# First operands loaded from one array in the order of use, on one queue, in smaller pieces; warming matmuls on a program constant

## The chip, the cores and the metric

The kernel runs on one core of one Trainium2 chip. The metric is the device time of one execution in microseconds (us), lower is better. It was run three times before the change: 705.35, 705.52 and 707.34 us, median 705.52.

## What is computed

`x` has 2048 rows (the sequence) and 512 columns. Two branches of `x` are mixed by a gate per row:

```python
g = sigmoid((x * gate_w).sum(-1, keepdims=True))
# branch A: the real part of a DFT over columns and then over rows, as matrix products
a = einsum("bsd,ed->bse", x, dft_hid_re);  b = einsum("bsd,ed->bse", x, dft_hid_im)
A = einsum("ts,bse->bte", dft_seq_re, a) - einsum("ts,bse->bte", dft_seq_im, b)
# branch B: a gated MLP of width 1376
B = einsum("bsf,fd->bsd", silu(x @ w1) * (x @ w3), w2)
out = g * A + (1 - g) * B
```

All inputs and the output are float32.

## The kernel before

Every product of matrices is made as three matmuls of 128x128 by 128x512: each operand is split into a high part (rounded to the matmul's format, names ending in `h`) and a low part (what is left, names ending in `l`), and high times high, high times low and low times high are added up in PSUM. ScalarE (ACT in the profile) makes the high part by a copy (L63), VectorE (DVE) the low part by a subtraction (L64). Matrices are cut into 2x2 blocks `B11` to `B22`, and seven products of sums of blocks, `P1` to `P7`, take the place of eight. The program has three large stages. First the DFT over the columns (PSUM tiles `dP`): `DSEQ` lists its 14 products, seven for each half `g` of the sequence, and begins with `P2` of half 0 and `P2` of half 1. Both need only the block `B21` of `x` (tiles `xB21_0` and `xB21_1`) and the block `B21` of the DFT matrix (`dB21`). Then comes the MLP (`X`, `Y`, `Z`), and last the DFT over the rows (`P`), whose end writes `out`.

A block is a tile of 128 partitions by 1024 numbers: two halves of 512, `q` = 0 and 1, which are the two steps of 128 of the contraction. `sums_of(s, (0,), True)` multiplies the first halves alone, before the second halves have arrived; with `first` set it runs all four matmuls of high by high, then the four of low by high, then the four of high by low, so that the low parts may come later (L186). Without it, each of the four row blocks takes its three matmuls in turn through `mm3` (L71). A matmul row in the profile reads "stationary names are the second, moving names the first": in `dP<-dB21h,x0B21h` four blocks of 128 columns of `x0B21h` are loaded in turn as weights, and 512 columns of `dB21h` are streamed through each.

The start of the program is what the change touches. `load_d("B21", ...)` loads `dB21` in two halves, the first on ACT's DMA queue, the second on SP's; `load_x(g, "B21", 2)` loads `xB21_0` and `xB21_1` in two halves each on SP's queue. On SP the order is: x0 first half, x1 first half, d second half, x0 second half, x1 second half, then the other blocks as whole tiles of 512 KB. The arrays lie in device memory as rows of 1024 numbers per partition, so a half is 128 pieces of 2 KB, 4 KB apart. While these loads run, TensorE has nothing of its own to do and multiplies a tile of zeros, `warm`, nine times (L793); VectorE fills that tile first (L790). Then the first half of `xB21_0` is split by VectorE alone (L114, L115), the others by ACT and VectorE in the order d, x1, d, x0, x1. Engines take their instructions in the order in which the program issues them; `keep_in_program_order` pins the order of the DMAs.

Of the kernel before, what the change touches and what calls it, by code (L numbers as in the profile page):

```python
# [16 lines left out]
G = 2  # L17
NC = (F + P - 1) // P
NP = (NC - 1) // 2
NQ = 4  # L20
WARM = 9


@with_exitstack
def fnet_swiglu_gate_kernel(
    ctx: ExitStack,
    tc: tile.TileContext,
    xt: bass.AP,
    cc: bass.AP,
    dd: bass.AP,  # L30
# [10 lines left out]
    nc = tc.nc  # L41
# [20 lines left out]
    def split(hi, lo, src):  # L62
        nc.scalar.activation(hi, src, AF.Copy)  # L63
        nc.vector.tensor_sub(lo, src, hi.bitcast(F32))  # L64

    def minus_sum(o, a, b):
        nc.vector.scalar_tensor_tensor(o, a, -1.0, b, op0=ALU.mult, op1=ALU.subtract)

    def mm3(ps, ah, al, bh, bl, first, last, chain=False):
        for n, (u, v) in enumerate(((ah, bh), (ah, bl), (al, bh))):  # L70
            nc.tensor.matmul(ps, u, v, start=first and n == 0, stop=last and n == 2,  # L71
                             skip_group_check=chain)
# [14 lines left out]
    act0 = const.tile([P, 24], F32, tag="act0", name="act0")  # L87
# [1 line left out]


    RX, RD, XF, WD = {}, {}, {}, {}
    XK = ("B11", "B21", "B12", "B22")

    def load_x(g, k, parts=1):
        RX[g, k] = raw(f"x{k}_{g}")
        for a in range(parts):
            n = slice(a * 1024 // parts, (a + 1) * 1024 // parts)
            yield tc.keep_in_program_order(nc.sync.dma_start(RX[g, k][:, n], xt[g, XK.index(k)][:, n]))

    def load_d(k, queues=(nc.sync,)):  # L100
        RD[k] = raw(f"d{k}")
        w = 1024 // len(queues)
        for a, queue in enumerate(queues):
            n = slice(a * w, (a + 1) * w)
            yield tc.keep_in_program_order(queue.dma_start(RD[k][:, n], dd[XK.index(k)][:, n]))

    def operand(src, name, parts=1, pool=op):
        tag = {op: "op", zo: "zo", f4: "f4"}[pool]
        h, l = (pool.tile([P, 1024], F32R, tag=tag, name=f"{name}{v}") for v in "hl")

        def piece(a, by_vector=False):
            n = slice(a * 1024 // parts, (a + 1) * 1024 // parts)
            if by_vector:
                nc.vector.tensor_copy(h[:, n], src[:, n])  # L114
# [4 lines left out]
        return (half(h), half(l)), [lambda a=a, **kw: piece(a, **kw) for a in range(parts)]  # L119

    def form_x(g, k, parts=1):
        r = {n: RX.get((g, n)) for n in ("B11", "B12", "B21", "B22", "F2", "F3")}
        if k == "F3":
            RX[g, k] = raw(f"xF3_{g}")
            nc.vector.tensor_add(RX[g, k], r["B12"], r["B22"])
# [9 lines left out]
        XF[g, k], pieces = operand(RX[g, k], f"x{g}{k}", parts)  # L135
        return pieces

    def form_d(k, parts=1):
        r = {n: RD.get(n) for n in ("B11", "B12", "B21", "B22", "v5", "v6")}
        if k == "v5":  # L140
            RD[k] = raw("dv5")
            nc.vector.tensor_sub(RD[k], r["B11"], r["B12"])
# [9 lines left out]
        WD[k], pieces = operand(RD[k], f"d{k}", parts, f4 if k in ("B22", "v4") else zo)  # L152
        return pieces

    PX = {"P2": ("B21", "B21"), "P1": ("B11", "B11"), "P5": ("F3", "v5"), "P6": ("F2", "v6"),
# [3 lines left out]
    def forms_of(s):  # L159

        if s < len(DSEQ):
            g, (xk, dk) = DSEQ[s][0], PX[DSEQ[s][1]]
            todo = form_x(g, xk) + (form_d(dk) if dk not in WD else [])
            for f in todo:
                f()

# [5 lines left out]
    def sums_of(s, qs=(0, 1), first=False):  # L172
        g, p = DSEQ[s]
        x, z = ((0, 1), (2, 3)) if g == 0 else ((2, 3), (0, 1))
        own = p in ("P1", "P2", "P5")
        if own and 0 in qs:
            ks = x if p == "P1" else z
            DP[g, p] = [pair(k, f"d{p}{g}{k}") for k in ks]
        ps = DP[g, {"P6": "P1", "P7": "P1", "P4": "P1", "P3": "P5"}.get(p, p)]
        xh, xl = XF[g, PX[p][0]]  # L180
        wh, wl = WD[PX[p][1]]
        if first:

            for n, (u, v) in enumerate(((xh, wh), (xl, wh), (xh, wl))):
                for i in range(4):
                    nc.tensor.matmul(ps[i // 2][:, i % 2], u[:, 0, i * P : (i + 1) * P], v[:, 0],  # L186
                                     start=n == 0, stop=False, skip_group_check=True)
# [38 lines left out]
    def load_w(c):  # L226
        WS[c] = raw(f"ws{c}")
        nc.sync.dma_start(WS[c], w13[c])

    def prep_wa(c):  # L230
        h, l = (zo.tile([P, 768], F32R, tag="zo", name=f"wa{c}{v}") for v in "hl")
        split(h, l, WS[c][:, :768])
        WA[c] = half(h, 3), half(l, 3)

    def sum_wb(c):
        w = half(WS[c], 4)
        u = raw(f"wu{c}")
# [222 lines left out]
    todo = list(INNER)  # L460
# [315 lines left out]

    def run(*gens):
        for gen in gens:  # L780
            for _ in gen:
                pass
# [7 lines left out]
    nc.vector.memset(warm, 0.0)  # L790
    wps = pair(0, "wps")
    for n in range(WARM):
        nc.tensor.matmul(wps[:, 0], warm[:, :P], warm, start=True, stop=True)  # L793
    nc.scalar.activation(act0[:, :1], warm[:, :1], AF.Silu)
    run(load_x(0, "B11"), load_d("B11"), load_x(0, "B12"), load_x(0, "B22"),
        load_d("B12"), load_d("B22"))
# [16 lines left out]
    def work(count):  # L813
        for _ in range(count):
            if later:
                later.pop(0)()

    tasks = {2: lambda: run(load_x(1, "B11")), 3: lambda: run(load_x(1, "B12")),
             5: lambda: run(load_x(1, "B22")), 6: lambda: run(load_x(1, "B21")),
             7: lambda: load_w(0), 9: lambda: sum_wb(0), 11: lambda: prep_wa(0),  # L820
             12: lambda: (prep_wb(0), load_w(1))}
# [65 lines left out]
    start = AT[2, "P1", 0]  # L887
# [73 lines left out]
```

## Time and profile before

| what | value |
|---|---|
| median of three runs | 705.52 us (705.35 to 707.34) |
| the profiled execution, its own time | 707.5 us |
| span of that execution, first to last instruction | 705.7 us |
| PE (matmuls) busy, share of the span | 699.7 us, 99% |
| VectorE busy | 565.1 us, 80% |
| ScalarE busy | 345.8 us, 49% |
| DMA over the span | 193.25 MB, mean 274 GB/s |
| first matmul on loaded data starts | 6.25 us |
| last matmul starts | 701.53 us |

A row of the timeline has the start, the duration (from the first start to the last end of merged rows), the engine (a `q` behind it marks the issue of a DMA on that engine's queue), the line, the operation, and what it writes and reads; in brackets stand the idle time before it and what ended that. A matmul's own record, about 389 ns, is longer than the distance to the next one's start, since matmuls are pipelined: their pace is read from the starts.

### The profile page before, as it was taken

How to read it: one execution, taken by the hardware profiler on the slowest of the kernel's cores; microseconds unless marked ns; L12 is line 12 of the kernel's file. 1: busy time of each engine (PE TensorE's matmuls, PEld its weight loads, DVE VectorE, ACT ScalarE, POOL GpSimd, SP SyncE). 2: the span in 40 equal slices, each digit the busy share in tenths (PEclk: the TensorE clock that was granted, in tenths of full speed). 3: DMA queues.
4: the chain of work that ended last, by engine and by line, in shares of the span. 5: the costliest groups of instructions: out<-in, count | busy, mean ns of one | idle time of the engine just before them, and what ended most of it. 6: DMA issues, size and time to landing. Idle time of an engine off the chain costs nothing.

```text
span 705.7 us, 8651 instructions
## 1 busy us (share of the span) xinstructions
PE 699.7 (99%) x3069; PEld 576.5 (82%) x3069; DVE 565.1 (80%) x606; ACT 345.8 (49%) x390; POOL 95.9 (14%) x154
## 2 busy tenths in 40 slices
PE   8999999999999999999999999999999999999997
PEld 5888888888888888888888888888888888888886
DVE  5898756877878986769968998779486976999886
ACT  4746444555455555565353466435443445445531
POOL 0013302222222222100100001000000020110110
PEclk9999999999999999999999999999999999999999
DMA  8377966788898889889988878916899969798923
GB/s 300 117 255 277 393 240 235 292 304 312 306 326 297 300 318 370 303 295 401 401 323 289 279 267 232 328 62 215 290 347 370 354 126 279 205 336 253 233 32 89
DMA packets 58458, 193.25 MB, mean 274 GB/s; under 512 B 6252, under 2 KB 6508, under 8 KB 58416
## 3 DMA queue, kind: packets, MB, share of 16 engines
q1 hardware_dynamic: 36432, 116.54, 46.7%
q0 software_dynamic: 21696, 75.78, 32.5%
q8 instruction: 24, 0.39, 0.2%
q10 hardware_dynamic: 288, 0.39, 0.2%
q14 instruction: 18, 0.15, 0.1%
HBM read 124.78 MB, written 67.90 MB: 273 GB/s over the span
## 4 chain that ended last, share of the span: by engine, by line
PE 99%; DMA 1%; ACT 0%; DVE 0%; DVEq 0%; issue 0%
PE P L71 54%; PE X L71 17%; PE dP L71 10%; PE Z L71 8%; PE Y L71 4%; PE Lx L71 3%; PE last L71 1%; DMA dB<-dd 1%; PE dP L186 1%; ACT dB21h L63 0%; DVE uP L669 0%; DVEq L957 0%
## 5 line engine op out<-in xcount | busy, mean ns | idle before, releaser
L63 ACT ACTIVATE zh<-B 128x1024 fp32r<-128x1024 f32 x146 | 148.5, 1020 | 183.4 <-PE P L71 146.2
L64 DVE TENSOR_TENSOR zl<-B,zh 128x1024 fp32r<-128x1024 f32 x146 | 169.9, 1170 | 50.8 <-ACT zh L63 46.1
L71 PE MATMUL P<-zh,a2P 128*128 128x512 f32 x368 | 115.3, 389 | 0.0
L530 DVE TENSOR_TENSOR B<-B,B 128x1024 f32<-128x1024 f32 (+1 forms) x76 | 87.6, 1164 | 1.9 <-DMA B<-hsp 1.5
L71 PE MATMUL P<-zh,a0P 128*128 128x512 f32 x280 | 87.5, 389 | 0.0
L71 PEld LDWEIGHTS P<-zh,a2P 128*128 128x128 f32 x368 | 69.1, 188 | 14.3
L71 PE MATMUL P<-zh,a1P 128*128 128x512 f32 x256 | 79.2, 389 | 0.0
L71 PE MATMUL P<-zl,a2P 128*128 128x512 f32 x184 | 71.6, 389 | 0.0
L71 PEld LDWEIGHTS P<-zh,a0P 128*128 128x128 f32 x280 | 52.6, 188 | 10.9
L71 PE MATMUL P<-zh,f1P 128*128 128x512 f32 x192 | 59.4, 389 | 0.0
L71 PEld LDWEIGHTS P<-zh,a1P 128*128 128x128 f32 x256 | 48.0, 188 | 9.9
L71 PE MATMUL P<-zl,a0P 128*128 128x512 f32 x140 | 54.5, 389 | 0.0
L71 PE MATMUL P<-zl,a1P 128*128 128x512 f32 x128 | 49.8, 389 | 0.0
L71 PEld LDWEIGHTS P<-zh,f1P 128*128 128x128 f32 x192 | 36.0, 188 | 7.5
L71 PEld LDWEIGHTS P<-zl,a2P 128*128 128x128 f32 x184 | 34.5, 188 | 7.2
L71 PE MATMUL P<-zl,f1P 128*128 128x512 f32 x96 | 37.3, 389 | 0.0
L71 PEld LDWEIGHTS P<-zl,a0P 128*128 128x128 f32 x140 | 26.3, 188 | 5.5
L71 PEld LDWEIGHTS P<-zl,a1P 128*128 128x128 f32 x128 | 24.0, 188 | 5.0
L63 ACT ACTIVATE zh<-LB 128x1024 fp32r<-128x1024 f32 x14 | 14.9, 1062 | 20.4 <-PE P L71 18.2
L772 DVE TENSOR_TENSOR uP<-uP,P 128x1024 f32<-128x1024 f32 x16 | 19.5, 1219 | 4.3 <-PE P L71 4.3
L71 PEld LDWEIGHTS P<-zl,f1P 128*128 128x128 f32 x96 | 18.0, 188 | 3.8
L64 DVE TENSOR_TENSOR zl<-LB,zh 128x1024 fp32r<-128x1024 f32 x14 | 17.1, 1220 | 4.4 <-ACT zh L63 4.4
(1282 smaller groups left out, 1408.4 us busy)
## 6 DMA issues: line engine op xcount, KB each, us to landing
B<-cc SPq DMA_DIRECT2D x56, 512.0 KB, 6.1
r<-ab SPq DMA_DIRECT2D x24, 512.0 KB, 6.0
fsp<-f2P POOLq DMA_DIRECT2D x24, 512.0 KB, 4.4
a2P<-fsp SPq DMA_DIRECT2D x24, 512.0 KB, 7.1
hsp<-u POOLq DMA_DIRECT2D x20, 512.0 KB, 5.9
fsp<-f1P POOLq DMA_DIRECT2D x16, 512.0 KB, 4.8
B<-hsp SPq DMA_DIRECT2D x16, 512.0 KB, 10.3
a1P<-fsp SPq DMA_DIRECT2D x16, 512.0 KB, 8.1
```

Of the source, the lines that this page charges most:

```text
L63: nc.scalar.activation(hi, src, AF.Copy)
L64: nc.vector.tensor_sub(lo, src, hi.bitcast(F32))
L71: nc.tensor.matmul(ps, u, v, start=first and n == 0, stop=last and n == 2, skip_group_check=chain)
L186: nc.tensor.matmul(ps[i // 2][:, i % 2], u[:, 0, i * P : (i + 1) * P], v[:, 0], start=n == 0, stop=False, skip_group_check=True)
L530: nc.vector.tensor_add(t, t, RAW[b, o, q])
L772: nc.vector.tensor_add(flat(t), flat(t), flat(whole))
```

## The change

The three `B21` blocks move into a new input array, `head`, written on the host in the order in which the pieces are loaded. `HEAD` lists the pieces as (tile, half, first column in the half, width): x0 and d first halves in two pieces of 256 columns each, alternating, then the first half of x1, the second half of d, the second half of x0, the second half of x1. Each piece is contiguous in device memory, 128 KB or 256 KB, and all are loaded on SP's queue. The first two pieces are made into high parts by VectorE, the later ones by ACT; the low parts follow on VectorE. For the very first product the four matmuls of high by high become eight: all four weights by the first 256 columns of d, then all four by the other 256. The `first` order is now used for x1's first half too. The warming matmuls are fifteen of 256 columns instead of nine of 512, and read the program's constant 1.0 instead of a zeroed tile. The block `B21` of half 1, which is loaded once more later, comes in two DMAs.

The core of the diff:

```diff
-WARM = 9
+WARM = 15
+HEAD = ((0, 0, 0, 256), ("d", 0, 0, 256), (0, 0, 256, 256), ("d", 0, 256, 256),
+        (1, 0, 0, 512), ("d", 1, 0, 512), (0, 1, 0, 512), (1, 1, 0, 512))
...
+    def load_head(to, which, only=None):
+        o = 0
+        for k, q, c, w in HEAD:
+            if k == which and only in (None, (q, c)):
+                n = slice(q * 512 + c, q * 512 + c + w)
+                tc.keep_in_program_order(
+                    nc.sync.dma_start(to[:, n], head[o : o + P * w].rearrange("(p n) -> p n", p=P)))
+            o += P * w
...
-        def piece(a, by_vector=False):
-            n = slice(a * 1024 // parts, (a + 1) * 1024 // parts)
+        def one(n=slice(0, 1024), by_vector=False):
             if by_vector:
-                nc.vector.tensor_copy(h[:, n], src[:, n])
-                nc.vector.tensor_sub(l[:, n], src[:, n], h[:, n].bitcast(F32))
-            else:
-                split(h[:, n], l[:, n], src[:, n])
+                return nc.vector.tensor_copy(h[:, n], src[:, n])
+            return nc.scalar.activation(h[:, n], src[:, n], AF.Copy)
+
+        def two(n=slice(0, 1024)):
+            return nc.vector.tensor_sub(l[:, n], src[:, n], h[:, n].bitcast(F32))
...
-            for n, (u, v) in enumerate(((xh, wh), (xl, wh), (xh, wl))):
+            whole = ((xh, wh, 0, 512), (xl, wh, 0, 512), (xh, wl, 0, 512))
+            parts = ((xh, wh, 0, 256), (xh, wh, 256, 256), *whole[1:]) if s == 0 else whole
+            for n, (u, v, c, w) in enumerate(parts):
                 for i in range(4):
-                    nc.tensor.matmul(ps[i // 2][:, i % 2], u[:, 0, i * P : (i + 1) * P], v[:, 0],
-                                     start=n == 0, stop=False, skip_group_check=True)
+                    tc.keep_in_program_order(nc.tensor.matmul(
+                        ps[i // 2][:, i % 2, c : c + w], u[:, 0, i * P : (i + 1) * P], v[:, 0, c : c + w],
+                        start=n == 0, stop=False, skip_group_check=True))
...
-    dg, xg = load_d("B21", (nc.scalar, nc.sync)), [load_x(g, "B21", 2) for g in range(G)]
-    next(dg)
-    next(xg[0])
-    next(xg[1])
-    run(dg, *xg)
-    warm = f4.tile([P, 512], mybir.dt.bfloat16, tag="f4", name="warm")
-    nc.vector.memset(warm, 0.0)
+    RX[0, "B21"], RX[1, "B21"], RD["B21"] = raw("xB21_0"), raw("xB21_1"), raw("dB21")
+    for k, q, c, w in HEAD:
+        load_head(RD["B21"] if k == "d" else RX[k, "B21"], k, (q, c))
+    ones = nc.const_aps.tensor(1.0, [P, 256], mybir.dt.bfloat16)
     wps = pair(0, "wps")
     for n in range(WARM):
-        nc.tensor.matmul(wps[:, 0], warm[:, :P], warm, start=True, stop=True)
-    nc.scalar.activation(act0[:, :1], warm[:, :1], AF.Silu)
...
-    x0, x1, d0 = form_x(0, "B21", 2), form_x(1, "B21", 2), form_d("B21", 2)
-    x0[0](by_vector=True)
-    for f in (d0[0], x1[0], d0[1], x0[1], x1[1]):
-        f()
+        nc.tensor.matmul(wps[:, 0, :256], ones[:, :P], ones, start=True, stop=True)
+    nc.scalar.activation(act0[:, :1], ones[:, :1], AF.Silu)
...
+    made = {0: form_x(0, "B21"), 1: form_x(1, "B21"), "d": form_d("B21")}
+    for n, (k, q, c, w) in enumerate(HEAD):
+        tc.keep_in_program_order(made[k][0](slice(q * 512 + c, q * 512 + c + w), n < 2))
+    for k, q, c, w in sorted(HEAD, key=lambda v: (v[1], (0, "d", 1).index(v[0]))):
+        tc.keep_in_program_order(made[k][1](slice(q * 512 + c, q * 512 + c + w)))
...
     sums_of(0, (0,), True)
-    sums_of(1, (0,))
+    sums_of(1, (0,), True)
```

What the program issues on SP's DMA queue at its start, before the change (`xB_0` and `xB_1` are the tiles of the two halves of the sequence, `dB` that of the DFT matrix):

```order
L98 DMA xB_0_85<-xt 128x512
L98 DMA xB_1_87<-xt 128x512
L105 DMA dB_83<-dd 128x512
L98 DMA xB_0_85<-xt 128x512
L98 DMA xB_1_87<-xt 128x512
L98 DMA xB_0_105<-xt 128x1024
```

And with it:

```order
L105 DMA xB_0_83<-head 128x256
L105 DMA dB_85<-head 128x256
L105 DMA xB_0_83<-head 128x256
L105 DMA dB_85<-head 128x256
L105 DMA xB_1_84<-head 128x512
L105 DMA dB_85<-head 128x512
L105 DMA xB_0_83<-head 128x512
L105 DMA xB_1_84<-head 128x512
L113 DMA xB_0_111<-xt 128x1024
```

Eight issues stand ahead of the first whole block instead of five, and the first half of d, which was the only DMA on ACT's queue here, is now the second and the fourth of them.

TensorE's real work at the start, before the change (`dP_143` and `dP_144` are the PSUM pairs of half 0, `dP_157` one of half 1):

```order
L186 MATMUL dP_143<-dB21h,x0B21h 128x512 x2
L186 MATMUL dP_144<-dB21h,x0B21h 128x512 x2
L186 MATMUL dP_143<-dB21h,x0B21l 128x512 x2
L186 MATMUL dP_144<-dB21h,x0B21l 128x512 x2
L186 MATMUL dP_143<-dB21l,x0B21h 128x512 x2
L186 MATMUL dP_144<-dB21l,x0B21h 128x512 x2
L71 MATMUL dP_157<-dB21h,x1B21h 128x512
L71 MATMUL dP_157<-dB21l,x1B21h 128x512
L71 MATMUL dP_157<-dB21h,x1B21l 128x512
```

And with it (`dP_153`, `dP_154` are half 0, `dP_171`, `dP_172` half 1):

```order
L202 MATMUL dP_153<-dB21h,x0B21h 128x256 x2
L202 MATMUL dP_154<-dB21h,x0B21h 128x256 x2
L202 MATMUL dP_153<-dB21h,x0B21h 128x256 x2
L202 MATMUL dP_154<-dB21h,x0B21h 128x256 x2
L202 MATMUL dP_153<-dB21h,x0B21l 128x512 x2
L202 MATMUL dP_154<-dB21h,x0B21l 128x512 x2
L202 MATMUL dP_153<-dB21l,x0B21h 128x512 x2
L202 MATMUL dP_154<-dB21l,x0B21h 128x512 x2
L202 MATMUL dP_171<-dB21h,x1B21h 128x512 x2
L202 MATMUL dP_172<-dB21h,x1B21h 128x512 x2
```

The first four matmuls of 512 columns are now eight of 256, and half 1 runs its four high by high matmuls before it needs a low part.

Behind the first halves the two programs have the same matmuls in the same order but for one, in the middle of `P1` of half 0 (PSUM pairs `dP_225` and `dP_226` before). Before the change it stands like this there:

```order
L71 MATMUL dP_225<-dB11h,x0B11h 128x512
L71 MATMUL dP_225<-dB11l,x0B11h 128x512
L71 MATMUL dP_225<-dB11h,x0B11l 128x512
L71 MATMUL dP_226<-dB11h,x0B11h 128x512
L71 MATMUL dP_226<-dB11l,x0B11h 128x512
```

And with it (the pairs are `dP_239` and `dP_240`, and `dP_281` belongs to `P5`):

```order
L76 MATMUL dP_239<-dB11h,x0B11h 128x512
L76 MATMUL dP_239<-dB11l,x0B11h 128x512
L76 MATMUL dP_239<-dB11h,x0B11l 128x512
L76 MATMUL dP_281<-dv5h,x0F3h 128x512
L76 MATMUL dP_240<-dB11h,x0B11h 128x512
L76 MATMUL dP_240<-dB11l,x0B11h 128x512
```

The first matmul of `P5`, which needs `dv5h` and `x0F3h` from ACT, now runs twelve matmuls earlier. On VectorE and ACT a few later neighbours change places, and POOL's program is the same.

More of the change, by code (lines that the diff above doesn't have):

```diff
@@ L27, in fnet_swiglu_gate_kernel @@
     tc: tile.TileContext,
+    head: bass.AP,
     xt: bass.AP,
@@ L107, in operand, with load_x @@
-    def operand(src, name, parts=1, pool=op):
+    XK = ("B11", "B12", "B22")
+    def load_head(to, which, only=None):
[6 more added lines that the diff above has]
+            o += P * w
+    def load_x(g, k):
+        RX[g, k] = raw(f"x{k}_{g}")
+        if k == "B21":
+            load_head(RX[g, k], g)
+        else:
+            tc.keep_in_program_order(nc.sync.dma_start(RX[g, k], xt[g, XK.index(k)]))
@@ L119, in operand, with form_x @@
-        return (half(h), half(l)), [lambda a=a, **kw: piece(a, **kw) for a in range(parts)]
-    def form_x(g, k, parts=1):
+                return nc.vector.tensor_copy(h[:, n], src[:, n])
+            return nc.scalar.activation(h[:, n], src[:, n], AF.Copy)
+        def two(n=slice(0, 1024)):
+            return nc.vector.tensor_sub(l[:, n], src[:, n], h[:, n].bitcast(F32))
+        return (half(h), half(l)), (one, two)
+    def form_x(g, k):
         r = {n: RX.get((g, n)) for n in ("B11", "B12", "B21", "B22", "F2", "F3")}
@@ L134, in form_x, with form_d @@
             nc.vector.tensor_add(r["B21"], r["F2"], r["B21"])
-        XF[g, k], pieces = operand(RX[g, k], f"x{g}{k}", parts)
+        XF[g, k], pieces = operand(RX[g, k], f"x{g}{k}")
         return pieces
-    def form_d(k, parts=1):
+    def form_d(k):
         r = {n: RD.get(n) for n in ("B11", "B12", "B21", "B22", "v5", "v6")}
@@ L151, in form_d @@
             minus_sum(r["B21"], r["v6"], r["B21"])
-        WD[k], pieces = operand(RD[k], f"d{k}", parts, f4 if k in ("B22", "v4") else zo)
+        WD[k], pieces = operand(RD[k], f"d{k}", f4 if k in ("B22", "v4") else zo)
         return pieces
@@ L162, in forms_of @@
             g, (xk, dk) = DSEQ[s][0], PX[DSEQ[s][1]]
-            todo = form_x(g, xk) + (form_d(dk) if dk not in WD else [])
+            todo = form_x(g, xk) + (form_d(dk) if dk not in WD else ())
             for f in todo:
@@ L775, in fnet_swiglu_gate_kernel @@
     LASTS = []
[L779 to L782, printed above, removed]
[L784 to L790 removed]
+    RX[0, "B21"], RX[1, "B21"], RD["B21"] = raw("xB21_0"), raw("xB21_1"), raw("dB21")
+    for k, q, c, w in HEAD:
+        load_head(RD["B21"] if k == "d" else RX[k, "B21"], k, (q, c))
+    ones = nc.const_aps.tensor(1.0, [P, 256], mybir.dt.bfloat16)
     wps = pair(0, "wps")
     for n in range(WARM):
[L793 to L800 removed]
+        nc.tensor.matmul(wps[:, 0, :256], ones[:, :P], ones, start=True, stop=True)
+    nc.scalar.activation(act0[:, :1], ones[:, :1], AF.Silu)
+    load_x(0, "B11")
+    load_d("B11")
+    load_x(0, "B12")
+    load_x(0, "B22")
+    load_d("B12")
+    load_d("B22")
+    made = {0: form_x(0, "B21"), 1: form_x(1, "B21"), "d": form_d("B21")}
[3 more added lines that the diff above has]
+        tc.keep_in_program_order(made[k][1](slice(q * 512 + c, q * 512 + c + w)))
     forms_of(2)
@@ L816, in work @@
                 later.pop(0)()
-    tasks = {2: lambda: run(load_x(1, "B11")), 3: lambda: run(load_x(1, "B12")),
-             5: lambda: run(load_x(1, "B22")), 6: lambda: run(load_x(1, "B21")),
+    tasks = {2: lambda: load_x(1, "B11"), 3: lambda: load_x(1, "B12"),
+             5: lambda: load_x(1, "B22"), 6: lambda: load_x(1, "B21"),
              7: lambda: load_w(0), 9: lambda: sum_wb(0), 11: lambda: prep_wa(0),
@@ L940 @@
         w2q[:, q, :, : v[0, 0].size] = v.reshape(2, P, -1)
+    dq = np.stack([re[0], re[1], im[0], im[1]]).reshape(4, P, 1024)
+    xq = xq.reshape(G, 4, P, 1024)
+    b21 = {0: xq[0, 1], 1: xq[1, 1], "d": dq[1]}
     arrays = {
-        "xt": xq.reshape(G, 4, P, 1024),
+        "head": np.concatenate([b21[k][:, q * 512 + c : q * 512 + c + w].reshape(-1) for k, q, c, w in HEAD]),
+        "xt": xq[:, (0, 2, 3)],
         "cc": np.stack(cb).reshape(2, G, 4, NQ, P, 1024),
-        "dd": np.stack([re[0], re[1], im[0], im[1]]).reshape(4, P, 1024),
+        "dd": dq[[0, 2, 3]],
         "w13": np.stack([wq[:, :, 0, 0], wq[:, :, 0, 1], wq[:, :, 1, 1], wq[:, :, 1, 0]], 2)
```

13 lines of the change are left out of this document (3 added, 10 removed).

## The prediction

> **What bounds the kernel now.** I read the table of waits first, for TensorE alone, then its busy time in long stretches, then the chain that ended last.
>
> ```profile
> PE wps L793 <- DVE warm L790: 1.2, 1, 1.2
> PE dP L186 <- ACT dB21h L63: 1.0, 1, 1.0
> 20.00:120.00 100.00, 100.00 (x443) 1.00 0.69 258
> 520.00:620.00 100.00, 100.00 (x443) 1.00 0.87 270
> 6.25 4.63 PE dP L186 x12
> 10.88 73.60 PE dP L71 x324
> 295.06 289.91 PE P L71 x1279
> ```
>
> TensorE waits twice in the whole program, both times before 6.25 us. A hundred us near the start and a hundred near the end hold the same 443 records (columns: stretch, its length, PE busy, count, granted clock, DMA share, GB/s), though the DMA share differs. In the chain 1279 matmuls took 289.91 us, 0.2267 us each. So TensorE's pace is the bound, and the time is: the start of the real work, plus 3060 real matmuls (12 + 324 of them in the first stage) at 0.2267, plus the end. What the other engines do costs nothing here unless it makes TensorE wait. The change can only move the start.
>
> The start itself, from the timeline:
>
> ```profile
> 0.74 0.40 ACTq L105 DMA_DIRECT2D dB<-dd  x1
> 0.74 0.86 SPq L98 DMA_DIRECT2D xB<-xt  x2
> 0.87 0.27 DVE L790 MEMSET warm<- 128x256 uint32 x1 [0.87 <-PEq L951]
> 1.19 4.02 PE L793 MATMUL wps<-warm 128*128 128x512 bf16 x9 [1.19 <-DVE warm L790]
> 5.39 0.43 DVE L114 CAST x0B21h<-xB 128x512 fp32r<-128x512 f32 x1 [4.25 <-DMA xB<-xt]
> 5.57 0.63 ACT L63 ACTIVATE dB21h<-dB 128x512 fp32r<-128x512 f32 x1 [2.90 <-DMA dB<-dd]
> 6.25 2.07 PE L186 MATMUL dP<-dB21h,x0B21h 128*128 128x512 f32 x4 [1.04 <-ACT dB21h L63]
> 8.13 1.83 PE L186 MATMUL dP<-dB21h,x0B21l 128*128 128x512 f32 x4
> 9.79 1.09 PE L186 MATMUL dP<-dB21l,x0B21h 128*128 128x512 f32 x4
> 10.72 0.40 PE L71 MATMUL dP<-dB21h,x1B21h 128*128 128x512 f32 x1
> L186 PE MATMUL dP<-dB21h,x0B21h x4: 628/628/795, 6.3 to 7.7; 128*128 128x512 f32 x4
> L186 PE MATMUL dP<-dB21h,x0B21l x4: 549/628/628, 8.1 to 9.4; 128*128 128x512 f32 x4
> L186 PE MATMUL dP<-dB21l,x0B21h x4: 387/395/397, 9.8 to 10.5; 128*128 128x512 f32 x4
> ```
>
> The loads decide 6.25: ACT idles until d has landed, splits it in 0.63, and TensorE follows. Then something is to be seen that the page's clock row (full throughout) does not show. The first eight real matmuls take 628 ns each and 9.79 - 6.25 = 3.54 us together; the next four 395 ns and 0.93 us, 0.2325 each. At full pace eight take 8 x 0.2267 = 1.81, so the slow pace cost 1.73. The nine warming matmuls (4.02 us) ran slowly too, 0.43 apart, and 1.04 idle us lie behind them. The slow pace ended at about 9.7, some 3.4 us of unbroken work after 6.25.
>
> I call **offset** the time at which the first real matmul would have started had all run at full pace: the thirteenth started at 10.72, so 10.72 - 12 x 0.2267 = 8.00 in this execution. Without the slow pace it would be 6.25. The profiled execution took 707.5 us; the three timed ones 705.35, 705.52 and 707.34. The gap of 2.0 is close to the 1.73, so I read (an inference) the two quick ones as executions in which the real work began at full pace: 705.45 goes with 6.25, 707.5 with 8.00.
>
> The Trainium skill, "TensorE: Matmul & The Clock Gate", Part 1, says that TensorE gets half of its clock until a free-running window of about 3.4 us has been busy, that the point varies from run to run, and that 512 columns are then 427 ns apart. The trace agrees: 0.43 in the warming matmuls, about 3.4 us of real work before the pace doubled.
>
> **The change part by part.** *Warming.* The first warming matmul waited for VectorE's fill (0.87 + 0.27). The constant is set by POOL long before:
>
> ```profile
> 0.32 0.10 POOL L951 MEMSET const-bfloat16-1.0<- 128x1 bf16 x1
> ```
>
> So the warming starts at about 0.9 instead of 1.19. Fifteen of 256 columns take 15 x 0.43 / 2 = 3.2 us: done at 4.1 instead of 5.2. They cost nothing as long as the data come later.
>
> *Loads.* These rows bound the landing of a 128 KB piece (queue, KB, us from issue to landing):
>
> ```profile
> xB<-xt SPq DMA_DIRECT2D x4, 256.0 KB, 5.2
> dB<-dd ACTq DMA_DIRECT2D x1, 256.0 KB, 4.8
> dB<-dd SPq DMA_DIRECT2D x1, 256.0 KB, 5.1
> out<-uP ACTq DMA_DIRECT2D x1, 128.0 KB, 1.9
> 1.75:2.50 0.75, 0.75 (x4) 0.20 (x2) 0.00 (x0) 0.74 (x2) 0.00 (x0) 1.00 0.63 175
> 2.50:3.50 1.00, 1.00 (x4) 0.40 (x3) 0.00 (x0) 0.17 (x1) 0.00 (x0) 1.00 0.88 303
> 3.50:4.25 0.75, 0.75 (x4) 0.25 (x2) 0.00 (x0) 0.00 (x0) 0.00 (x0) 1.00 0.82 172
> ```
>
> An issue on SP takes 0.43 (two in 0.86), so the pieces go out at 0.74, 1.17, 1.60 and 2.03. The lower bound is 1.9, the store of 128 KB at the end with nothing beside it; the upper is 4.8 to 5.1, 256 KB in the crowd of the start. What decides between them is the data rate: bytes began to move at 1.75, at 175, 303 and 172 GB/s in the three stretches (last column), 0.131, 0.434 and 0.563 MB in all by their ends. The first 256 KB of x0 and of d, 0.52 MB, had been moved by about 4.0, and the engines took them up at 5.39 and 5.57: some 1.4 us behind the bytes. In the order of use the first two pieces (0.26 MB) have moved by about 2.9 and all four by 4.0. I take 1.3 and 1.2 behind the bytes, a little less since a piece is half as long: 4.2 and 5.2, nearer to the rows of the start than to the store.
>
> *Splitting.* VectorE copies 512 columns in 0.43, so 256 in about 0.25: high x0 and high d of the first pieces are there at 4.45, and the first real matmul starts at 4.5, 1.75 earlier. The fourth piece goes through ACT (half of 0.63 and some overhead, 0.4), and the second four can start at 5.6.
>
> *Eight matmuls for four.* A matmul of 256 columns streams half as long but loads the same weights:
>
> ```profile
> L186 PEld LDWEIGHTS dP<-dB21h,x0B21h x4: 288/330/333, 6.3 to 7.3; 128*128 128x128 f32 x4
> L186 PEld LDWEIGHTS dP<-dB21l,x0B21h x4: 187/188/330, 9.4 to 10.3; 128*128 128x128 f32 x4
> ```
>
> A load is 188 ns at full pace and 330 at the slow one, against 113 and 213 for 256 columns. Bounds for the eight at full pace: 0.91 if only columns count, 1.81 if each costs a whole step of 0.2267. I take the weight load, 8 x 0.188 = 1.5, so the split costs 0.6; slowly 8 x 0.33 = 2.64, against 4 x 0.43 = 1.7.
>
> *Sum.* At full pace: four from 4.5 to 5.25, a pause, four from 5.6 to 6.35, and that is as far as four old matmuls: offset 6.35 - 4 x 0.2267 = 5.45. At the slow pace until the third group is done: 4.5 to 5.82, on to 7.14, four at 0.43 to 8.85; offset 8.85 - 8 x 0.2267 = 7.0. The warming and the pieces leave only short breaks, so I expect the pace to rise somewhere between, and take 5.9. Against the quick runs: 705.45 - (6.25 - 5.9) = 705.1; against the profiled execution: 707.5 - (8.00 - 5.9) = 705.4. I forecast **705.2**; its own range, by offsets 5.45 to 7.0, is 704.6 to 706.3.
>
> *What is late next.* If TensorE starts 2 us earlier, this is the first place where it could meet another engine:
>
> ```profile
> 13.81 1.23 DVE L125 TENSOR_TENSOR xF<-xB,xB 128x1024 f32<-128x1024 f32 x1 [0.31 <-DMA xB<-xt]
> 15.01 1.23 DVE L142 TENSOR_TENSOR dv<-dB,dB 128x1024 f32<-128x1024 f32 x1
> 17.74 1.03 ACT L206 ACTIVATE dt1P<-dP 128x1024 f32<-128x1024 f32 x1 [0.33 <-PE dP L71]
> 20.56 1.02 ACT L206 ACTIVATE dt1P<-dP 128x1024 f32<-128x1024 f32 x1
> 21.63 0.19 PEld L71 LDWEIGHTS dP<-dB11h,x0B11h 128*128 128x128 f32 x1 [0.21 <-ACT dt1P L206]
> ```
>
> The second half of `P1` waits for ACT's second copy, done at 21.58; TensorE was there at 21.63, no slack at all. ACT's four steps up to it (copy, `x0F3h`, `dv5h`, copy) begin when TensorE has finished a sum (17.74), so they move with it. They are held only by the loads through `dv`, ready at 16.24: two steps more, 2 x 1.05, make 18.3, and TensorE needs them at offset + 60 x 0.2267. The moved matmul of `P5` fills one step more. So below an offset of about 4.5 the rest of the gain stays in this wait; 5.9 is clear of it by 1.4. The eighth DMA ahead of the whole blocks and ACT's freed issue change neither bytes nor path. VectorE's extra copy replaces work of ACT.
>
> **Rivals.** *Faster than the bound.* Differences under 0.3% (2.1 us) are what a measurement of this kernel cannot tell from none. If the pieces land like the store at the end, d's second at 2.03 + 2.0, and 256 columns cost half, the eight run from 4.2, just behind the warming, to 5.1: offset 4.2, held at 4.5 by ACT: 705.45 - 1.75 = 703.7. Or the two quick runs owe their 2 us to something else and have the slow pace too: then 5.9 is to be set against 8.00 and gives 705.45 - 2.1 = 703.35. For the second speaks only that nothing in the profile shows a quick run. 0.2 in all.
>
> *The slow pace lasts longer, which makes it slower.* The mechanism: matmuls run at half pace until about 3.4 us have passed without a break, counted from some point that the program doesn't set. The old warming lasted 4.02; the new one lasts 3.2, less than that, and breaks off 0.4 before the real work. If the count starts with the real work at 4.5, the pace rises between 4.5 + 3.45 = 7.95 and 3.4 later, 11.4. At the middle, 9.7: four old matmuls by 7.14, six more at 0.43, and 9.7 - 10 x 0.2267 = 7.4: 705.45 + 1.15 = 706.6. At 11.4 the offset is 8.2 and the time 707.4. Against it: two of three runs seem to have started at full pace with 1.04 us of idle time before them. It counts as slower by over 0.3% only where the pace rises after about 12. 0.2, of which 0.1 beyond the bound. The page on the clock gate named above gives this rule; by it a warming shorter than the window cannot open the gate alone.
>
> *The loads come no earlier.* If the fourth piece, now third in line behind x0 and d on one queue, lands like the d half on SP did, 2.03 + 4.8 = 6.8, the second four start at 7.2 and end at 7.95: offset 7.05, 706.3. For it: the bytes ahead of it are the same 0.52 MB. 0.1.
>
> The Trainium skill, "DMA: Bandwidth & Descriptors", Anatomy of one DMA, gives 2.0 us plus bytes over 436 GB/s (for GpSimd's queue), an estimate of 2.3 for 128 KB. The old 256 KB halves would by that take 2.6, and took 4.8 and more here; by its figure the sum would be near the first rival's 703.7.
>
> **How the numbers follow.** Forecast 0.5, inside the bound; faster rivals 0.2; the lasting slow pace 0.2; late loads 0.1. Of the last two 0.12 lie beyond 707.6. So faster 0.2, same 0.68, slower 0.12. The range takes in the first rival's lower price and most of the slow pace: 703.3 to 707.2.
>
> **What would show it.** The first real matmul near 4.5; the second four near 5.6 behind ACT; the records of 256-column matmuls about 0.19 apart, or 0.33 if slow; the durations 628 or 389 telling where the pace rises; 443 records per hundred us as before; no wait of TensorE after 25 us. I am wrong if the last matmul's start, less 3059 steps, gives an offset outside 5.4 to 7.0, or if TensorE waits anywhere later.

## The result and the profile after

The changed kernel takes 705.11 us (median of 22 runs, 704.58 to 706.72); the kernel before, run beside it, 705.71 (22 runs, 705.32 to 707.92). The ratio is 0.9983, 95% interval 0.9976 to 0.9991: it compares means, 705.20 to 706.38 here. So the change is a little faster, by 0.17%; that is inside the bound of 0.3% and counts as the same. The times of before stand in two groups, twelve of 22 at 705.3 to 705.8 and ten at 707.2 to 707.9. Those of the changed kernel stand in one, 704.6 to 705.7, with a single 706.72. Most of the difference of the means comes from the upper group of before: its twelve quick times have a mean of 705.47, 0.27 above that of the changed kernel. The profiled execution took 705.4 us, its span 703.6.

The table of waits of the changed kernel, TensorE alone, and its busy time in two long stretches:

```profile
PE wps L802 <- PEq L970: 0.8, 1, 0.8
20.00:120.00 100.00, 100.00 (x441) 1.00 0.70 263
520.00:620.00 100.00, 100.00 (x443) 1.00 0.86 268
```

The long wait for data is gone from this table; what is left in it is the program's own start. Short waits don't show in it where matmul records overlap: those of weight loads, below, have to be read from the timeline. The pace behind the start is the old one. Its timeline at the start:

```profile
0.78 3.35 PE L802 MATMUL wps<-const-bfloat16-1.0 128*128 128x256 bf16 x15 [0.78 <-PEq L970]
2.79 0.29 DVE L126 CAST x0B21h<-xB 128x256 fp32r<-128x256 f32 x1 [2.79 <-DMA xB<-head]
3.39 0.29 DVE L126 CAST dB21h<-dB 128x256 fp32r<-128x256 f32 x1 [0.30 <-DMA dB<-head]
3.79 2.24 PE L202 MATMUL dP<-dB21h,x0B21h 128*128 128x256 f32 x8
4.14 0.42 ACT L127 ACTIVATE x0B21h<-xB 128x256 fp32r<-128x256 f32 x1 [1.90 <-DMA xB<-head]
4.52 0.42 ACT L127 ACTIVATE dB21h<-dB 128x256 fp32r<-128x256 f32 x1
5.87 1.08 PE L202 MATMUL dP<-dB21h,x0B21l 128*128 128x512 f32 x4
6.78 1.07 PE L202 MATMUL dP<-dB21l,x0B21h 128*128 128x512 f32 x4
```

The first real matmul starts at 3.79 instead of 6.25, and the first group of 512 columns (5.87 to 6.78, 0.2275 each) already runs at full pace. The durations show where the pace rose:

```profile
L202 PEld LDWEIGHTS dP<-dB21h,x0B21h x8: 188/323/338, 3.7 to 5.6; 128*128 128x128 f32 x8
L202 PE MATMUL dP<-dB21h,x0B21h x8: 283/415/582, 3.8 to 5.7; 128*128 128x256 f32 x8
L202 PE MATMUL dP<-dB21h,x0B21l x4: 389/391/395, 5.9 to 6.6; 128*128 128x512 f32 x4
```

Most of the eight narrow matmuls were slow (weight loads of 323 ns in the median), the last of them not (188). There is a short wait among them as well: the third starts at 4.61, 0.46 behind the second, when ACT's copy of x0's second piece is done (4.14 to 4.56). The offset is 5.87 - 4 x 0.2267 = 4.96, against 8.00 in the profiled execution before: 3.04 us earlier. But the last matmul starts here:

```profile
699.18 0.39 PE L76 MATMUL last<-zh,a2P 128*128 128x512 f32 x1
```

699.18 - 3059 x 0.226667 = 5.81 (the step with two more digits, since it is taken 3059 times). The offset of the kernel before grew from 8.00 to 8.16 over its length; the changed one from 4.96 to 5.81, so 0.85 us were given back on the way. The timeline shows three places, all of them weight loads that waited for a copy by ACT:

```profile
12.14 1.06 ACT L127 ACTIVATE dB11h<-dB 128x1024 fp32r<-128x1024 f32 x1 [0.22 <-DMA dB<-dd]
13.11 1.92 ACT L223 ACTIVATE dt0P<-dP 128x1024 f32<-128x1024 f32 x2
14.77 1.23 DVE L138 TENSOR_TENSOR xF<-xB,xB 128x1024 f32<-128x1024 f32 x1 [0.31 <-DMA xB<-xt]
14.91 1.03 ACT L223 ACTIVATE dt1P<-dP 128x1024 f32<-128x1024 f32 x1
16.00 0.19 PEld L76 LDWEIGHTS dP<-dB11h,x0B11h 128*128 128x128 f32 x1 [0.41 <-ACT dt1P L223]
17.24 1.06 ACT L127 ACTIVATE dv5h<-dv 128x1024 fp32r<-128x1024 f32 x1
18.20 1.01 ACT L223 ACTIVATE dt1P<-dP 128x1024 f32<-128x1024 f32 x1
19.26 0.19 PEld L76 LDWEIGHTS dP<-dB11h,x0B11h 128*128 128x128 f32 x1 [0.45 <-ACT dt1P L223]
21.78 1.06 ACT L127 ACTIVATE x0F2h<-xF 128x1024 fp32r<-128x1024 f32 x1 [2.56 <-DVE xF L141]
32.88 0.19 PEld L76 LDWEIGHTS dP<-dv7h,x0F1h 128*128 128x128 f32 x1 [0.37 <-ACT dt0P L223]
```

The idle time in brackets is that of the weight load; matmuls run on for part of it. By the starts of the matmuls the offset grows by 0.27 at 16.00, by 0.31 at 19.26 and by 0.23 at 32.88; the rest is drift. All three places go back to whole blocks that came late. The first: `dB11h` starts at 12.14 (before: 11.18), behind its DMA, so ACT's copies for the first two sums run behind it without a pause until 15.9, and the first half of `P1` waits for the third of them. The second: `xF`, the first sum of whole blocks, starts 0.96 later than before (14.77, then 13.81; in e11, a second profile of the same kernel, 14.10), ACT works through `x0F3h` and `dv5h` behind it, and the copy that frees PSUM for the second half of `P1` ends at 19.2, when TensorE is already there. The third: VectorE's work behind `xF` moves with it, `x0F2h` on ACT starts at 21.78 (e4, below: 20.58), and a copy further on is late.

The end of the program has changed too, though the edit doesn't touch it. The time less the end offset is 699.34 before (707.5 - 8.16) and 699.59 now (705.4 - 5.81), 0.25 more. The records of SP's waits at the end show where: after the last store SP goes through a list of waits for DMAs, about 0.06 us each; once that store has landed, six more of them follow in the changed kernel, and one before. What sets the order of this list stays open.

### The profile page after: what moved, and what is told of

The parts are those of the page before. It is cut to its first block, busy times and chain, and to the rows that moved or that the text cites. A ratio compares the mean times of both kernels' runs of the same rounds, so it can differ in the third digit from the quotient of the medians.

```text
span 703.6 us, 8676 instructions
## 1 busy us (share of the span) xinstructions
PE 698.7 (99%) x3079; PEld 577.2 (82%) x3079; DVE 564.9 (80%) x608; ACT 345.7 (49%) x391; POOL 96.1 (14%) x154
## 4 chain that ended last, share of the span: by engine, by line
PE 99%; DMA 0%; SPq 0%; ACT 0%; DVE 0%; DVEq 0%; issue 0%
PE P L76 55%; PE X L76 17%; PE dP L76 10%; PE Z L76 9%; PE Y L76 4%; PE Lx L76 3%; PE dP L202 1%; PE last L76 1%; DMA xB<-head 0%; SPq L105 0%; ACT x0B21h L127 0%; DVE uP L686 0%; DVEq L976 0%
```

## The experiments

Each was timed beside the kernel before, in three sets: e1, e2, e3 and e9; e4 to e7; e8 and e10 to e12. Offsets are worked out as above, "start" from the first matmuls of 512 columns that run at full pace, "end" from the last matmul, both of the one profiled execution; "break" is TensorE's idle time between warming and real work in it.

| kernel | median us | lowest, highest | runs above 705.9 | break | offset start, end | xF starts |
|---|---|---|---|---|---|---|
| before | 705.49 to 705.71 by set | 704.96, 707.96 | see below | 1.04 | 8.00, 8.16 | 13.81 |
| changed | 705.11 | 704.58, 706.72 | 1 of 22 | 0 | 4.96, 5.81 | 14.77 |
| e1 loads alone | 705.29 | 704.59, 705.61 | 0 of 11 | 0 | 5.62, 5.70 | 14.64 |
| e2 warming alone | 706.87 | 705.03, 708.60 | 8 of 12 | 1.61 | 5.88, 5.96 | - |
| e3 before, longer warming | 705.90 | 705.53, 706.63 | 5 of 11 | 0 | 5.92, 6.50 | 13.55 |
| e9 changed, no warming | 706.00 | 705.53, 706.93 | 8 of 11 | 2.57 | 6.21, 6.30 | 13.97 |
| e4 whole first halves | 704.40 | 704.05, 706.27 | 2 of 12 | 0.53 | 4.79, 4.86 | 13.56 |
| e5 ACT's copies first | 704.80 | 704.50, 705.24 | 0 of 11 | 0 | 4.54, 4.93 | 14.33 |
| e6 d on ACT's queue | 704.77 | 704.19, 705.20 | 0 of 11 | 0 | 4.53, 4.61 | 13.31 |
| e7 half 1 in the old order | 705.00 | 704.37, 705.39 | 0 of 11 | 0 | 4.69, 5.30 | - |
| e11 changed again | 705.23 | 704.73, 705.78 | 0 of 11 | 0 | 4.52, 5.14 | 14.10 |
| e12 as e4, again | 704.33 | 704.04, 706.70 | 3 of 11 | 0.55 | 7.06, 7.13 | 13.23 |
| e8 whole halves, copies first | 704.52 | 704.07, 706.51 | 2 of 12 | 0.43 | 4.63, 4.85 | 13.30 |
| e10 whole halves, two queues | 706.11 | 704.16, 706.59 | 7 of 11 | 0.68 | 4.94, 5.00 | 12.77 |

Runs of before above 707 were 10 of 22 beside the changed kernel, and 3, 7 and 7 of 35 in the three sets of the experiments.

### Which part makes the gain, and what the two groups of before are

**e1, the loads without the new warming.**

```diff
-WARM = 15
+WARM = 9
-    ones = nc.const_aps.tensor(1.0, [P, 256], mybir.dt.bfloat16)
+    warm = f4.tile([P, 512], mybir.dt.bfloat16, tag="f4", name="warm")
+    nc.vector.memset(warm, 0.0)
...
-        nc.tensor.matmul(wps[:, 0, :256], ones[:, :P], ones, start=True, stop=True)
+        nc.tensor.matmul(wps[:, 0], warm[:, :P], warm, start=True, stop=True)
```

> The changed kernel with the warming of before (nine matmuls of 512 columns on a tile zeroed by VectorE). Theory (the time is the start of the real work plus a fixed 3060 steps, and the pace rises once about 3.4 us of TensorE work have passed without a long break): the warming runs from 1.2 to about 5.2 and the real work follows with no break, its data being there since 4.9; offset 5.2 to 5.9 instead of 4.96, one group of times, 705.1 to 705.8, none near 707.4. Rival (the shorter warming on the constant makes the gain): two groups, near 705.5 and 707.4, as before.

Measured: 705.29, one group. The real work begins at 4.65, late by the longer warming, and its offset is 5.62 instead of 4.96; but nothing is given back (end 5.70), so the end differs from the changed kernel's by 0.1. So the loads alone bring the earlier end offset (the quick e2, with the old loads, has 5.96), and no run lies in a second group without the new warming. In the times little of it is left: the ratio to the kernel before in this set is 0.9997 (0.9988 to 1.0005), and the 0.25 of the longer end works against it.

**e2, the new warming without the loads.** The opposite edit in the kernel before: fifteen matmuls of 256 columns on the constant, the loads as they were.

> The kernel before with only the warming of the change (fifteen of 256 columns on the constant). Theory: the data still come at 6.25 and the warming ends at 4.1, a break of 2.1 us instead of 1.0, so the slow pace holds in most executions: most times 707 to 708, median above 707. Rival (the two groups of the kernel before have nothing to do with the warming, but with loads): the two groups as before, about half and half.

Measured: four times at 705.0 to 705.3, eight at 706.5 to 708.6, median 706.87; of the kernel before, 3 of 35 in the same set lay above 707. By itself this half of the change makes the kernel slower (ratio 1.0017, 1.0006 to 1.0029). It makes the break longer and the warming shorter (3.4 us instead of 4.0) at once; the two were not taken apart. The profile caught one of the quick executions; its break, from the table of waits, beside the first group of real matmuls:

```profile
PE dP L186 <- ACT dB21h L63: 1.6, 1, 1.6
L186 PE MATMUL dP<-dB21h,x0B21h x4: 396/400/504, 5.7 to 6.6; 128*128 128x512 f32 x4
```

400 ns in the median: the real work began at full pace, which before was only inferred of the quick runs (the profiled execution of before has 628).

**e3, the kernel before with no break.**

```diff
-WARM = 9
+WARM = 12
```

> The kernel before with twelve warming matmuls instead of nine, which fill the time until the data are there (1.2 + 12 x 0.43 = 6.3). Theory: no break, so one group at 705.3 to 705.8 and none near 707.4, and in the profile the first real matmuls take about 390 ns, not 628. Rival (the groups come from the loads): both groups again, about half and half.

Measured: one group, 705.53 to 706.63, none at 707; the real matmuls take 395 ns in the median:

```profile
1.19 4.88 PE L793 MATMUL wps<-warm 128*128 128x512 bf16 x12 [1.19 <-DVE warm L790]
L186 PE MATMUL dP<-dB21h,x0B21h x4: 387/395/578, 5.7 to 6.6; 128*128 128x512 f32 x4
```

No run lies near 707, though with 3 of 35 there beside it, eleven without one are weak evidence; e2 and the later runs carry it. The median is 0.1 above what was expected: the offset starts at 5.92 and grows to 6.50. This is not what a quick start costs the old kernel, since e2, as quick, goes from 5.88 to 5.96. In e3 `x0F3h` stands ahead of ACT's first copy for `P1` (15.22 and 16.17), in e2 and before behind it, so the edit changed the order on ACT too, and `P1` waits for that copy.

**e9, the changed kernel with a single warming matmul.**

```diff
-    for n in range(WARM):
-        nc.tensor.matmul(wps[:, 0, :256], ones[:, :P], ones, start=True, stop=True)
+    nc.tensor.matmul(wps[:, 0, :256], ones[:, :P], ones, start=True, stop=True)
```

> The changed kernel with one warming matmul instead of fifteen. Theory: the first real matmul still starts at 3.8, but the pace rises only 3.4 to 6.8 us after that, at 7.2 to 10.6; offsets 6.2 to 7.9, times 705.9 to 707.6. Rival (the early pieces alone make the gain): as the changed kernel, 705.1 within 0.3.

Measured: 706.00, at the low end of what was expected, and 0.9 above the changed kernel. The first real matmul starts at 3.72 all the same; the eight narrow matmuls and the first four wide ones are slow:

```profile
L202 PE MATMUL dP<-dB21h,x0B21h x8: 415/415/582, 3.7 to 5.9; 128*128 128x256 f32 x8
L202 PE MATMUL dP<-dB21h,x0B21l x4: 628/628/628, 6.1 to 7.4; 128*128 128x512 f32 x4
```

The third and the fifth matmul wait for ACT's copies here too (they start at 4.48 and 5.10, the copies end at 4.44 and 5.05). Early data without a warmed TensorE are worth nothing here: 706.00 against 705.5 of the kernel before.

### Where the gain is given back

**e4, first halves in one piece.**

```diff
-HEAD = ((0, 0, 0, 256), ("d", 0, 0, 256), (0, 0, 256, 256), ("d", 0, 256, 256),
+HEAD = ((0, 0, 0, 512), ("d", 0, 0, 512),
         (1, 0, 0, 512), ("d", 1, 0, 512), (0, 1, 0, 512), (1, 1, 0, 512))
...
-            parts = ((xh, wh, 0, 256), (xh, wh, 256, 256), *whole[1:]) if s == 0 else whole
+            parts = whole
```

> The changed kernel with the first halves of x0 and d in one piece of 256 KB each, and four matmuls of 512 columns for the eight of 256. Theory (the eight cost as much as eight weight loads, so the split gains a start and pays it back): first real matmul at 4.3 to 4.7 instead of 3.8, but offset 4.4 to 5.0, time within 0.3 of the changed kernel. Rival (the small pieces make the gain): the halves land as late as before, first real matmul at 5.4 or later, 705.6 to 706.2.

Measured: 704.40, better than the changed kernel by more than either theory said. In its timeline:

```profile
3.46 0.43 DVE L126 CAST x0B21h<-xB 128x512 fp32r<-128x512 f32 x1 [3.46 <-DMA xB<-head]
4.18 0.43 DVE L126 CAST dB21h<-dB 128x512 fp32r<-128x512 f32 x1 [0.30 <-DMA dB<-head]
4.67 1.20 PE L202 MATMUL dP<-dB21h,x0B21h 128*128 128x512 f32 x4 [0.53 <-DVE dB21h L126]
13.56 1.22 DVE L138 TENSOR_TENSOR xF<-xB,xB 128x1024 f32<-128x1024 f32 x1 [0.31 <-DMA xB<-xt]
```

The real work starts 0.88 later than in the changed kernel, but as four matmuls, and its offset is 4.79, between the 4.96 and 4.52 of the changed kernel's two profiles: cutting the first halves in two gains nothing at the start that can be told. With two DMAs less on SP the whole blocks go out from 3.55 instead of 4.50, `xF` starts 1.2 earlier, and nothing is given back (end 4.86). Not all of the lower time comes from this: the time less the end offset is 699.23 (704.09 - 4.86), 0.36 less than in the changed kernel, since no wait of SP is left behind the last store's. All four versions with whole halves have this shorter end (699.2), all seven with small pieces the longer one (699.6).

**e5, ACT's two copies ahead of the next operands.**

```diff
         taken(n)
-        forms_of(n + 3)
+        if n == 1:
+            forms_of(3)
+        if n:
+            forms_of(n + 3)
...
-                nc.scalar.activation(hi(t), fl, AF.Copy, scale=-1.0 if p in ("P5", "P4") else 1.0)
+                c = nc.scalar.activation(hi(t), fl, AF.Copy, scale=-1.0 if p in ("P5", "P4") else 1.0)
+                if s < 2:
+                    tc.keep_in_program_order(c)
```

> The changed kernel with both of ACT's copies of the second product ahead of x0F3h and dv5h on ACT. Theory (part of the gain is given back in P1, which waits for the second copy behind the late blocks): TensorE no longer waits between the two halves of P1, the offset grows by 0.3 less, time 704.6 to 704.9. Rival (the wait moves on to the first matmul of P5, whose operands now come one copy later): 705.1 as the changed kernel.

Measured: 704.80. The offset grows by 0.39 (in the changed kernel 0.85 and, in its second profile, 0.62). The two copies now run in a row, from 14.48 to 16.68, before TensorE needs the second. What is left is mostly the first place, which the edit doesn't move: the offset is 4.57 ahead of `P1` and 4.80 behind its second matmul. It is 4.85 on both sides of the first matmul of `P5` (21.18), so the wait did not move there, as the rival had it; another 0.08 is lost at the third place. The edit also puts that matmul of `P5` back behind `P1`.

**e6, d's first half on ACT's queue.** Two DMAs less on SP, with the small pieces kept:

```diff
-                    nc.sync.dma_start(to[:, n], head[o : o + P * w].rearrange("(p n) -> p n", p=P)))
+                    (nc.scalar if which == "d" and q == 0 else nc.sync).dma_start(
+                        to[:, n], head[o : o + P * w].rearrange("(p n) -> p n", p=P)))
...
-    nc.scalar.activation(act0[:, :1], ones[:, :1], AF.Silu)
+    tc.keep_in_program_order(nc.scalar.activation(act0[:, :1], ones[:, :1], AF.Silu))
```

> The changed kernel with the two pieces of d's first half issued on ACT's queue instead of SP's. Theory (issues of 0.43 to 0.47 us on one queue set when the pieces land and when the whole blocks follow): the fourth piece goes out at about 1.2 instead of 2.1 and the whole blocks 0.9 earlier; second four matmuls 0.2 to 0.5 earlier, xF less late than 14.77, time 704.6 to 704.9. Rival (two queues share the same engines, and what is not needed first takes their time): the first piece lands later, 705.1 to 705.6.

Measured: 704.77. The start is not earlier (first real matmul 4.05, and offset 4.53, as e11's 4.52): the first pieces land later when both queues move at once.

```profile
3.50 0.29 DVE L126 CAST x0B21h<-xB 128x256 fp32r<-128x256 f32 x1 [3.50 <-DMA xB<-head]
13.31 1.23 DVE L138 TENSOR_TENSOR xF<-xB,xB 128x1024 f32<-128x1024 f32 x1 [0.31 <-DMA xB<-xt]
```

What it saves is behind: whole blocks from 3.54, `xF` at 13.31, and the offset grows by 0.08 only. The order of work on the four compute engines and the long end (704.23 - 4.61 = 699.6) are those of the changed kernel, so what it gains, 0.34 in the median against another set, comes from the queues alone. e4 and e6 take two issues off SP in different ways, and both end the giving back.

**e7, half 1's first halves in the old order.**

```diff
-    sums_of(1, (0,), True)
+    sums_of(1, (0,))
```

> The changed kernel with half 1's first halves in the old order (each row block takes its three matmuls in turn). Theory: x1's low part is there at 7.6, the third matmul that needs it starts at 8.1, so nothing waits: 705.1 within 0.2. Rival (the new order of half 1 hides a late low part): 0.2 to 0.5 slower.

Measured: 705.00. This part of the change does nothing that can be told.

### Putting them together

> The changed kernel once more, for comparison on the same chip with the three that follow. Both theories: 704.6 to 705.7, median 705.1.

Measured: 705.23; the comparison for the next three.

> The kernel of e4 (first halves in one piece) once more, beside the changed kernel. Theory (two issues less put the whole blocks 0.9 earlier, so nothing is given back in P1): 0.4 to 0.9 below the changed kernel of this call. Rival (e4's lower time was the chip or chance): within 0.2 of it.

Measured: 704.33, 0.90 below the changed kernel of the same set, so e4's time was no chance; about 0.36 of this is the shorter end. Three of eleven runs lie at 706.3 to 706.7, and the profile caught one of these:

```profile
4.69 2.08 PE L202 MATMUL dP<-dB21h,x0B21h 128*128 128x512 f32 x4 [0.55 <-DVE dB21h L126]
L202 PE MATMUL dP<-dB21h,x0B21l x4: 632/632/632, 6.6 to 7.8; 128*128 128x512 f32 x4
L202 PE MATMUL dP<-dB21l,x0B21h x4: 402/606/632, 8.3 to 9.5; 128*128 128x512 f32 x4
```

The same kernel as e4, with real work from the same time (4.69, then 4.67), a break of 0.55, and slow matmuls until about 9.5: offset 7.06 instead of 4.79 and 706.39 us instead of 704.09. So the two groups are one program with two paces at its start, shown here on one kernel.

**e8**, the edits of e4 and e5 together.

> Whole first halves as in e4, and ACT's copies ahead as in e5. Theory (in e4 TensorE waits nowhere behind the first product, so there is nothing left for the order on ACT to save): as e4, within 0.2. Rival (the two gains add up): 0.2 to 0.4 below e4.

Measured: 704.52, as e4 and e12: nothing left to save there.

**e10**, the edits of e4 and e6 together.

> Whole first halves as in e4, with d's first half on ACT's queue as in e6. Theory (x0 and d now move at the same time and x1 joins in behind x0, so both land later than x0 in e4 but d about when it did, 4.2): first real matmul within 0.3 of e4's 4.67, time within 0.3 of e4. Rival (one queue in the order of use is what lands d early): d lands 0.5 to 1.0 later, 0.5 to 1.0 above e4.

Measured: median 706.11, which neither theory gave. The data came as the theory said (first real matmul at 4.82, and a quick execution at 704.21). But the break is 0.68, and seven of eleven runs lie at 706.0 to 706.6. The expectation left the pace out.

The best median is that of e4's version, 704.33 to 704.40. By the mean, which the executions above 705.9 raise, it is no better than e6: ratio to the kernel before 0.9982 and 0.9983, e6 0.9982, the changed kernel 0.9983 and 0.9991. The executions above 705.9 should go if its warming reached to 4.7; that was not tried.

## Why the prediction was right, and where by luck

The time forecast, 705.2, is 0.1 from the median, and the class was right. Step by step:

- **What bounds the kernel** was right: the pace is the old one, and the times less the end offset are 699.2 to 699.6 in all the profiled executions. The sum took "the end" as fixed, though; it is 0.25 longer in the changed kernel.
- **The slow pace as the cause of the two groups of times** was an inference; e2's quick profile and the pair e4 and e12 show the two paces, e9 what the slow one costs. No quick execution of the kernel before itself was profiled.
- **The warming** went as said: from 0.78 to 4.13, against 0.9 to 4.1.
- **The landing of the pieces was mis-sized.** I put the first d piece at 4.2 and the fourth piece at 5.2, "nearer to the rows of the start than to the store". This view of the changed kernel's DMAs gives the us from issue to landing:

```profile
xB<-head SPq DMA_DIRECT2D x2, 128.0 KB, 2.2
dB<-head SPq DMA_DIRECT2D x2, 128.0 KB, 2.3
```

  They landed at 3.4 and by 4.5. The store at the end, 1.9, was the better guide. The delay of 1.4 behind the bytes, read from the old loads, did not carry over: by 3.00 the DMA engines had moved 0.28 MB, and the second piece was taken up at 3.39; by 4.00 they had moved 0.53 MB, and the fourth was taken up at 4.52 without a wait. In the old loads the 0.52 MB by 4.0 need not have been x0's and d's, since x1's half was under way too.
- **Eight matmuls for four** had the wrong cause. I took a weight load each, 0.188 or 0.33. But narrow matmuls that wait for nothing start 0.213 apart at the slow pace (e1: 5.23, 5.44, 5.65, 5.87, 6.08) and 0.12 at the full one (e6: 5.08, 5.20, 5.32), half a wide one's step each time, while the weight loads take 330 and 188 ns beside them: the split itself costs next to nothing. In e9, slow throughout, the eight still take 2.40 (3.72 to 6.12) against 4 x 0.43 = 1.7, because they start before all pieces are there and wait for ACT's copies. The third matmul needs x0's second piece, which the sum left out. The extra 0.7, forecast as 0.9, is near by luck; it is about what the early start had gained, and e4 shows the exchange directly.
- **"What is late next"** named the right place and the wrong price. I held it clear for any offset above 4.5, from `dv` ready at 16.24, and wrote that the eighth DMA ahead of the whole blocks changed "neither bytes nor path". It changes when the blocks are issued, 4.50 instead of 2.97; `xF` came at 14.77, `dv5h` could start only at 17.24, and the copy behind them held TensorE. The reckoning itself holds with the later `dv`: two steps from 17.24 end at 19.2, which moves the bound from about 4.5 to about 5.4. Two other places bit that were not named, the first half of `P1` and 32.88. This step failed, and cost 0.85 in the profiled execution, 0.31 of it at the place named. The last sign given for being wrong, that TensorE waits anywhere later, came true.
- **The two errors cancel.** Start offset forecast 5.9, measured 4.96; given back forecast 0, measured 0.85; sum 5.9 and 5.81. With the 0.25 of the end this makes the 705.4 of the profiled execution. In e11 it is 4.52, 0.62 and 0.25, and 704.75. The number is right for a reason that is half luck.
- **Of the rivals**, the lasting slow pace has the mechanism right and did not come here, where warming and real work meet without a break; e2, e9 and e10 are what it looks like. The late loads did not come. The first faster rival had the landing right and the price of 256 columns (half, where nothing waits), but missed the waits for the pieces and that the block loads move.

## What to carry to other kernels

Where TensorE sets the time, look at the durations of its first matmuls, not only at when they start: here the kernels whose warming reached the first real matmul without a break were the ones that stayed quick, and a change that brings data earlier or cuts the warming should keep that. An extra DMA on a queue costs its issue time to every load behind it; here two issues of 0.43 us more on SP, against e4 and e6, put the issue of the later blocks back by about 1 us and gave back part of the gain, and one piece of 256 KB did as well at the start as two of 128. When work starts earlier, check each later place without slack against the new times of its loads, not against the old ones. Where a gain is well under 1 us, compare the ends of the programs too: 0.36 us of the difference between e4 and the changed kernel stands behind the last matmul.

## What the runs showed of the hardware

- Even a short break after the warming goes with a slow pace in part of the executions: with none, 1 of 77 runs of the changed kernel, e1, e5, e6, e7 and e11 lay above 705.9 (e3, also with none, spreads from 705.5 to 706.6 in one group); with 0.43 to 0.55 us, 2 of 12, 2 of 12 and 3 of 11; with 0.68, 7 of 11; with 1.61, 8 of 12. The share doesn't follow the break alone: with 1.04 us behind the longer warming of the kernel before, 27 of 127 lay above 707. That the break decides is argued from these counts; the length of the warming was not varied alone. The Trainium skill, "TensorE: Matmul & The Clock Gate", Part 1, says that the clock is released by a free-running window of activity. That agrees with one program having two paces; how much idle time a window bears is seen only from these counts.
- The profile's granted clock reads 1.00 through both paces; only the durations (628 against 389 ns) and the distances between starts show the slow one.
- A matmul of 256 columns with a new weight each time costs about half of one of 512 where it waits for nothing: 0.12 against 0.2267 us at the full pace, 0.213 against 0.427 at the slow one. The records of its weight loads, 188 and 330 ns, are longer than these steps and don't set them.
- Loads from contiguous memory at an idle start land soon: 2.2 to 2.3 us for 128 KB, and in e4 the first 256 KB at 3.46, 2.7 us after its issue, where the old half took 4.6. The Trainium skill, "DMA: Bandwidth & Descriptors", Anatomy of one DMA, has a fit for GpSimd's queue, which makes an estimate of 2.3 and 2.6. These loads on SP's queue agree with it. Whether order, queue or contiguity brought this was not taken apart; in e10, contiguous but on two queues, the first half landed at 4.00.
